# Attention and feed-forward on one core: padded 128-row scores against 64-row scores of two heads side by side

## The chip, the cores and the metric

The kernel runs on one core of a Trainium2 chip. The metric is the time of one execution on the device in microseconds (us); the median of 3 runs before the change is 449.39 us (449.11 to 452.02). Engines are named as in the profile: PE is TensorE (matmuls; PEld its weight loads), DVE is VectorE, ACT is ScalarE, POOL is GpSimd, and SP issues most transfers (DMA).

## The reference

The input is q, k, v of 8 batches, 12 heads, 448 positions, 64 columns (float32), two gains of 64, and two weights. What is computed:

```python
def rmsnorm(x, g):
    rms = np.sqrt(np.mean(x * x, axis=-1, keepdims=True) + 1e-06)
    return x / rms * g
q_n, k_n = rmsnorm(q, g_q), rmsnorm(k, g_k)
scores = (1 / 8) * q_n @ k_n.transpose(0, 1, 3, 2)
attn = softmax(scores)                      # over the keys
x = (attn @ v)  as 3584 tokens x 768        # 12 heads of 64 side by side
h = x @ w_in                                # 768 x 2048
out = (h * clip(h + 3, 0, 6) / 6) @ w_out   # 2048 x 768
```

## The kernel before

**Pairs.** Two heads, A and B, are one pair; a batch has 6, and there are 48 pairs. The 448 keys of a head are three tiles of 128 and a rest of 64. The rests of A and B share one tile, so a pair has seven key tiles: 0 to 2 of A, 3 with both rests, 4 to 6 of B.

**A pair's way.** k, q and v are loaded for two pairs at a time (`load_k`, `load_q`, `load_v`, into three rings). `square`, `stats_sum` and `stats_rstd` give the reciprocal norms on POOL or ACT, on DVE and on ACT. The first 14 pairs (`TD = 14`) are normalized on POOL or DVE (`normalize`, L333), transposed by PE (`transposes`, L349) into a PSUM tile, and copied out: `put_q` (L385, DVE or ACT) with the gains multiplied in, and `put_k` (L390) in two DVE copies of 64 rows. The later 34 pairs are normalized on POOL into a staging tile that the weights' loads have left free (`normalize_k`, L359, two operations; `normalize_q`, L367), transposed by a DMA that SP issues (`transposes_dma`, L378), and scaled by ACT (`scale_q`, L375).

**Padded k.** The transposed q of a pair holds A's 64 columns on rows 0 to 63 and B's on rows 64 to 127. The transposed k, `kpad`, has seven blocks of 128 columns. A block of A has k on rows 0 to 63 and zeros below, a block of B zeros above, the shared block both. So a score (`score`, L393) is a matmul over all 128 rows for every tile, and the zeros take the other head out. Zeros are written once (`clear_k`, `clear_kq`).

**From scores to x.** Scores go to two PSUM banks in turn; ACT makes the exponential of each (`expo`, L399) into one of 14 buffers. `weigh` (L413, L419) runs when all seven exponentials of a pair are there: in two halves, for each of four query tiles, it sums seven products with v, which has a column of ones for the denominators (the shared tile with both heads at once, 130 columns; the others 65). DVE divides (`divide`, L428, L429). The result is transposed by PE and copied by DVE (`x_out`, L446, `put_x`, L457) or, from pair 14, by DMA (L450).

**Feed-forward.** A batch whose six pairs are done gives 16 tiles of h, six matmuls of 448 columns each (`h_mm`, L461), a relu on ACT (L467) and a gate on DVE (L472), and then outputs of 16 matmuls of 384 columns (`y_mm`, L480) that ACT or DVE copies out (L280). L280 is the line of a helper, `copy`, that also casts v and the weights.

**What sets the order.** A planner in the kernel (`Plan`) plays the program through with a price for each operation on each engine that may run it, and writes out the instructions of every engine in the order that comes of it. An operation is ready a fixed time after those that it depends on; among ready ones the smallest key goes first. On PE, matmuls of attention and of the feed-forward share the time by credits; after 110 us of planned time PE's operations are put 500 ns behind what they need from other engines. Each engine then runs its own list in order, and waits on semaphores where the data asks for it.

Of the kernel before, what the change touches and what calls it, by code (L numbers as in the profile page):

```python
# [8 lines left out]
FP32 = mybir.dt.float32  # L9
BF16 = mybir.dt.bfloat16  # L10
# [35 lines left out]
class Plan:  # L46
# [52 lines left out]

    def begin(self, op, engine, ns, fn, now):  # L100
        fn()
        self.free[engine] = now + ns
        op.end = now + ns + op.lag
# [54 lines left out]
def kernel(  # L158
# [15 lines left out]
    P = 128  # L174
# [32 lines left out]
    k_st = ring(NS, [P, GP, 2, 5, D], FP32, "k_st")  # L207
    v_st = ring(NS, [P, GP, 2, 4, D], FP32, "v_st")
    vaug = ring(NV, [P, 4, 2, D + 1], BF16, "vaug")
    kq_r = ring(NK, [P, 11 * P], BF16, "kq")  # L210
    kpad = [x[:, 0:7 * P] for x in kq_r]
# [5 lines left out]
    qT_r = [x[:, 7 * P:7 * P + S] for x in kq_r]  # L217
# [7 lines left out]
    KQ = 11 * P // 2  # L225
# [37 lines left out]
    def load_k(eng, p, n):  # L263
        g, pr = part_of(p, n)
        src, st = heads(k, p, n), k_st[g][:, pr]
        eng.dma_start(
            out=st.rearrange("p r h t d -> p (r h) (t d)")[:, :, 0:NT * D], in_=blocks(src))
        for rows, x, t, rest in zip((lo, hi), (0, 0), (NT, 4), halves_of(src)):
            eng.dma_start(out=st[rows, :, x, t, :], in_=rest)
# [34 lines left out]
    def raw(a, p, n):  # L304

        g, pr = part_of(p, n)
        return (k_st, q_st)[a][g][:, pr].rearrange("p r h t d -> p r (h t) d")[:, :, 0:8, :]

    def square(eng, a, p, n, m):
        x = raw(a, p, n).rearrange("p r s d -> p r (s d)")  # L310
        sq = sq_r[m][:, 0:n].rearrange("p r s d -> p r (s d)")
# [20 lines left out]
    def normalize(eng, p, a):  # L332
        eng.tensor_tensor(  # L333
            out=qk_r[p % NQ][:, a].rearrange("p t h d -> p h t d"),
            in0=raw(a, p, 1).rearrange("p r (h t) d -> p (r h) t d", h=2),
# [19 lines left out]
    def normalize_k(eng, p):  # L355
        blocks = kq_st[p % NQ][:, 0:7 * P]
        for h in range(2):
            c0 = h * (NT * P)
            eng.tensor_tensor(  # L359
                out=blocks[:, c0:c0 + W4].rearrange("p (t c) -> p t c", t=4)[:, :, h * D:(h + 1) * D],  # L360
                in0=raw(0, p, 1)[:, 0, 4 * h:4 * h + 4, :],
                in1=rstd_r[(p // GP) % 2][:, 0, p % GP, 4 * h:4 * h + 4].unsqueeze(2)
                .to_broadcast([P, 4, D]), op=A_MULT,
            )

    def normalize_q(eng, p):
        eng.tensor_tensor(  # L367
            out=kq_st[p % NQ][:, 7 * P:11 * P].rearrange("p (t h d) -> p h t d", t=4, h=2),
            in0=raw(1, p, 1).rearrange("p r (h t) d -> p (r h) t d", h=2),
            in1=rstd_r[(p // GP) % 2][:, 1, p % GP, :].rearrange("p (h t) -> p h t", h=2)  # L370
            .unsqueeze(3).to_broadcast([P, 2, 4, D]), op=A_MULT,
        )

# [13 lines left out]
    def put_k(p, part):  # L387
        kp = kpad[p % NK]
        rows, c0 = ((lo, 0), (hi, NT * P))[part]
        nc.vector.tensor_copy(out=kp[rows, c0:c0 + 4 * P], in_=t_ps[rows, 0, :])  # L390

    def score(p, i, n):
        nc.tensor.matmul(  # L393
            out=sc_r[n % 2][:, 0:S], lhsT=kpad[p % NK][:, i * P:(i + 1) * P],
            rhs=qT_r[p % NK], start=True, stop=True,
        )
# [8 lines left out]
    def weigh(p, half):  # L405
        va = vaug[p % NV]
        e = {i: eT_r[(7 * p + n) % NE] for n, i in enumerate(ORDER)}
        for i in (2 * half, 2 * half + 1):


            c0 = i * P if (p // HP) % 2 == 0 else (i * P - P if i else S - P)
            cols = slice(c0, c0 + P)
            nc.tensor.matmul(  # L413
                out=av_ps[:, i, 0:2 * W], lhsT=e[3][:, cols], rhs=va[:, 3].rearrange("p h d -> p (h d)"),
                start=True, stop=False, skip_group_check=True,
            )
            for t in range(NT):
                for h in range(2):
                    nc.tensor.matmul(  # L419
                        out=av_ps[:, i, h * W:(h + 1) * W], lhsT=e[4 * h + t][:, cols],  # L420
                        rhs=va[:, t, h], start=False, stop=(t == NT - 1 and h == 1),
                        skip_group_check=True,
                    )
# [73 lines left out]
    def clear(eng, i):  # L497

        eng.memset(k_st[i][REST:P, :, 0, NT, :], 0.0)
        eng.memset(k_st[i][0:REST, :, 0, 4, :], 0.0)  # L500
# [5 lines left out]

    def clear_k(eng, i):
        eng.memset(kpad[i][D:P, 0:3 * P], 0.0)
        eng.memset(kpad[i][0:D, 4 * P:7 * P], 0.0)
# [15 lines left out]
    def clear_kq(eng, i):  # L525
        blocks = kq_st[i][:, 0:7 * P].rearrange("p (t c) -> p t c", c=P)
        eng.memset(blocks[:, 0:NT, D:P], 0.0)
        eng.memset(blocks[:, NT + 1:7, 0:D], 0.0)

# [6 lines left out]
    ORDER = (0, 1, 2, 3, 4, 5, 6)  # L536
# [9 lines left out]
    def x_stage(p):  # L546
        b = p // HP
        if p >= TD:
# [5 lines left out]
                      [div[p], at(px, p - 1)] + ([pq[p + 2], pk[2 * p + 4], pk[2 * p + 5]] if p >= HP else []),  # L554
                      165))
        px.append(add((p + 2, 1), [("DVE", 390, lambda: put_x(p))],
# [4 lines left out]
    def h_item(b, f):  # L561
# [7 lines left out]
        r = add((0, 0), [("ACT", 550, lambda: relu(it.bank[0], t))],  # L569
                [it.ops[-1]] + gate_ops[n - len(t_r):n - len(t_r) + 1] * (n >= len(t_r)))  # L570
        it.out = add((0, 0), [("DVE", 600, lambda: gate(b, f, it.bank[0], t))], [r])
# [217 lines left out]
```

## Time and profile before

| what | value |
|---|---|
| median of 3 runs | 449.39 us |
| profiled execution, span from the first to the last instruction | 449.5 us; the page gives no other time for it |
| first matmul begins, last one ends | 9.86 us, 445.76 us |
| scores, L393 | 336, 128 rows x 128, 448 columns, 359 ns each in the record |
| h, L461, and y, L480 | 768 and 896, 355 and 326 ns each in the record |
| values, L413 and L419 | 192 and 1152, 222 and 194 ns each in the record |
| exponentials on ACT, L399 | 336, 542 ns |
| granted PE clock, mean | 0.995 of full speed |

Matmuls are pipelined: the record of one reaches over the beginning of the next, so PE's busy time and the mean of a record say less than the distance from one beginning to the next. In the slices of the page a digit is the busy share of a fortieth of the span (11.2 us) in tenths. In the order of time a row begins with its start and its length in us; "x6" merges six equal instructions. In the table by stage the columns after the stage and its length are the busy us of PE, PEld, DVE, ACT and POOL with the number of instructions, then the granted clock, the DMA engines' share and GB/s. In the chain a row is start, length and what it was.

### The profile page before, as it was taken

How to read it: one execution, taken by the hardware profiler on the slowest of the kernel's cores; microseconds unless marked ns; L12 is line 12 of the kernel's file. 1: busy time of each engine (PE TensorE's matmuls, PEld its weight loads, DVE VectorE, ACT ScalarE, POOL GpSimd, SP SyncE). 2: the span in 40 equal slices, each digit the busy share in tenths (PEclk: the TensorE clock that was granted, in tenths of full speed). 3: DMA queues.
4: the chain of work that ended last, by engine and by line, in shares of the span. 5: the costliest groups of instructions: out<-in, count | busy, mean ns of one | idle time of the engine just before them, and what ended most of it. 6: DMA issues, size and time to landing. Idle time of an engine off the chain costs nothing.

```text
span 449.5 us, 9164 instructions
## 1 busy us (share of the span) xinstructions
PE 424.5 (94%) x3512; PEld 255.4 (57%) x3512; DVE 240.1 (53%) x428; ACT 274.8 (61%) x581; POOL 229.7 (51%) x251
## 2 busy tenths in 40 slices
PE   0888799899999989999999999999999999999996
PEld 0455366565566555666566565656565655555563
DVE  6899888845474346646444555453433253343321
ACT  2678678853487678878776777777767551132100
POOL 5899999958577766855667467552310000000000
PEclk9999899999999999999999999999999999999999
DMA  6899999981999999999899777955545210110021
GB/s 160 208 295 247 306 294 283 309 296 47 216 229 191 227 231 199 169 232 188 160 184 219 177 176 171 223 140 76 93 106 72 73 26 36 61 45 36 24 83 70
DMA packets 140908, 73.94 MB, mean 164 GB/s; under 512 B 90176, under 2 KB 137280, under 8 KB 140864
## 3 DMA queue, kind: packets, MB, share of 16 engines
q1 hardware_dynamic: 139232, 72.44, 69.3%
q10 hardware_dynamic: 1632, 0.92, 0.8%
q8 instruction: 27, 0.44, 0.4%
q14 instruction: 17, 0.14, 0.1%
HBM read 45.61 MB, written 11.01 MB: 126 GB/s over the span
## 4 chain that ended last, share of the span: by engine, by line
PE 84%; DMA 6%; POOL 2%; DVE 2%; ACT 2%; SPq 1%; issue 1%; POOLq 0%
PE m L461 29%; PE m L480 26%; PE sc L393 11%; PE av L419 7%; PE sc L480 5%; DMA k_st<-in_k_dram 4%; DMA kq<-w_st 3%; PE sc L461 3%; PE av L413 2%; ACT eT L399 2%; POOL qk L333 1%; POOL sq L315 1%; DVE vaug L280 1%; PE t_ps L349 1%; SPq L277 0%
## 5 line engine op out<-in xcount | busy, mean ns | idle before, releaser
L399 ACT ACTIVATE eT<-sc 128x448 bf16<-128x448 f32 x336 | 175.7, 542 | 48.6 <-PE sc L393 44.6
L461 PE MATMUL m<-xT,w_in_sb 128*128 128x448 bf16 x708 | 165.7, 355 | 0.2
L480 PE MATMUL m<-w_out_sb,gT 128*128 128x384 bf16 x768 | 150.0, 326 | 0.0
L393 PE MATMUL sc<-kq 128*128 128x448 bf16 x336 | 115.9, 359 | 8.2 <-ACT eT L399 6.4
L480 PEld LDWEIGHTS <-gT 128*128 128x128 bf16 x896 | 87.2, 98 | 62.3 <-issue 0.5
L461 PEld LDWEIGHTS <-w_in_sb 128*128 128x128 bf16 x768 | 74.1, 98 | 68.8 <-issue 6.0
L472 DVE SCALAR_TENSOR_TENSOR gT<-t_sb,m 128x448 bf16<-128x448 f32 x118 | 73.0, 620 | 72.9 <-ACT t_sb L467 72.4
L467 ACT ACTIVATE t_sb<-m 128x448 f32<-128x448 f32 x118 | 63.7, 541 | 47.3 <-PE m L461 44.3
L318 DVE TENSOR_REDUCE ssq<-sq 128x16 f32<-128x1024 f32 (+1 forms) x56 | 58.3, 1058 | 8.4 <-POOL sq L315 7.1
L359 POOL TENSOR_TENSOR w_st<-k_st,rstd 128x256 bf16<-128x256 f32 x68 | 40.2, 612 | 41.3 <-DMA kq<-w_st 40.6
L280 DVE COPY y_sb<-m 128x384 f32<-128x384 f32 x39 | 21.7, 557 | 61.4 <-PE m L480 61.2
L419 PE MATMUL av<-vaug,eT 128*128 128x65 bf16 x1152 | 54.5, 194 | 0.0
L419 PEld LDWEIGHTS <-eT 128*128 128x128 bf16 x1152 | 50.8, 99 | 4.4 <-issue 0.4
L315 POOL TENSOR_TENSOR sq<-k_st 128x1024 f32<-128x1024 f32 (+1 forms) x24 | 42.4, 1765 | 12.7 <-DMA k_st<-in_k_dram 5.9
L315 POOL TENSOR_TENSOR sq<-q_st 128x1024 f32<-128x1024 f32 (+1 forms) x26 | 44.5, 1710 | 7.1 <-DMA q_st<-in_q_dram 3.5
L393 PEld LDWEIGHTS <-kq 128*128 128x128 bf16 x336 | 31.3, 99 | 27.0 <-issue 4.9
L413 PE MATMUL av<-vaug,eT 128*128 128x130 bf16 x192 | 42.7, 222 | 0.0
L280 POOL CAST vaug<-v_st 128x512 bf16<-128x512 f32 x29 | 17.9, 618 | 45.2 <-PE av L419 44.6
L367 POOL TENSOR_TENSOR w_st<-q_st,rstd 128x512 bf16<-128x512 f32 x34 | 35.4, 1042 | 0.0
L429 DVE TENSOR_TENSOR xn<-av,rden 128x512 bf16<-128x512 f32 x48 | 33.2, 691 | 1.7
L428 DVE RECIPROCAL rden<-av 128x8 f32<-128x8 f32 x48 | 9.8, 205 | 34.1 <-PE av L419 33.7
L375 ACT ACTIVATE kq<-kq,gprime 128x448 bf16<-128x448 bf16 x34 | 22.6, 663 | 5.1 <-DMA kq<-w_st 5.1
(55 smaller groups left out, 222.5 us busy)
## 6 DMA issues: line engine op xcount, KB each, us to landing
out_dram<-y_sb SPq DMA_DIRECT2D x24, 384.0 KB, 2.9
k_st<-in_k_dram SPq DMA_DIRECT2D x23, 384.0 KB, 4.6
v_st<-in_v_dram SPq DMA_DIRECT2D x23, 384.0 KB, 4.6
q_st<-in_q_dram SPq DMA_DIRECT2D x22, 384.0 KB, 4.7
w_st<-in_moe_w_in_dram SPq DMA_DIRECT2D x8, 768.0 KB, 7.6
w_st<-in_moe_w_out_dram SPq DMA_DIRECT2D x8, 768.0 KB, 7.1
out_dram<-y_sb SPq DMA_DIRECT2D x8, 192.0 KB, 2.7
k_st<-in_k_dram SPq DMA_DIRECT2D x46, 32.0 KB, 3.9
```

Source lines behind the costliest of these rows:

```text
L280: (eng.copy if eng is nc.scalar else eng.tensor_copy)(out=out, in_=in_)
L315: eng.tensor_tensor(out=sq, in0=x, in1=x, op=A_MULT)
L318: nc.vector.tensor_reduce(out=ssq_r[(p // GP) % 2][:, a, p % GP:p % GP + n, :].rearrange("p r s -> p (r s)"), in_=sq_r[m][:, 0:n].rearrang ...
L359: eng.tensor_tensor(out=blocks[:, c0:c0 + W4].rearrange("p (t c) -> p t c", t=4)[:, :, h * D:(h + 1) * D], in0=raw(0, p, 1)[:, 0, 4 * h:4 ...
L393: nc.tensor.matmul(out=sc_r[n % 2][:, 0:S], lhsT=kpad[p % NK][:, i * P:(i + 1) * P], rhs=qT_r[p % NK], start=True, stop=True,)
L399: nc.scalar.activation(out=eT_r[n % NE][:, 0:S], in_=sc_r[n % 2][:, 0:S], func=EXP, bias=0.0, scale=1.0,)
L413: nc.tensor.matmul(out=av_ps[:, i, 0:2 * W], lhsT=e[3][:, cols], rhs=va[:, 3].rearrange("p h d -> p (h d)"), start=True, stop=False, skip_ ...
L419: nc.tensor.matmul(out=av_ps[:, i, h * W:(h + 1) * W], lhsT=e[4 * h + t][:, cols], rhs=va[:, t, h], start=False, stop=(t == NT - 1 and h = ...
L461: nc.tensor.matmul(out=m[:, 0:S], lhsT=w_in_sb[:, kt, f * P:(f + 1) * P], rhs=xT[:, kt, b % NX, x_slot(b)], start=(kt == 0), stop=(kt == N ...
L467: nc.scalar.activation(out=t[:], in_=m[:, 0:S], func=RELU, bias=0.5, scale=1.0 / 6.0,)
L472: nc.vector.scalar_tensor_tensor(out=gT[:, f, (b % 2) * S:(b % 2 + 1) * S], in0=t[:], scalar=1.0, in1=m[:, 0:S], op0=A_MIN, op1=A_MULT,)
L480: nc.tensor.matmul(out=m[:, 0:n], lhsT=gT[:, f, c0:c0 + P], rhs=w_out_sb[:, f, c:c + n], start=(f == 0), stop=(f == NFT - 1),)
```

## The change

k is no longer padded. Its transpose is four blocks of 128 columns, with A on rows 0 to 63 and B on rows 64 to 127, and the rests of both in the fourth. A score of A is a matmul over rows 0 to 63 alone, one of B over rows 64 to 127, and the shared tile over all. The order of the key tiles becomes shared, A0, B0, A1, B1, A2, B2. For pairs 14 to 47 the planner issues A's and B's score of one tile as one step into the two banks; for the first 14 pairs each score stays a step of its own. `weigh` handles one key tile for all four query tiles, so a pair's values are seven steps, each after its own exponential, in place of two after all seven. Scores have the first key on PE. `put_k` is one copy of 128 rows, on DVE or ACT; the late k is normalized in one operation; the clears of padding are gone; the transposing DMA moves 8 blocks in place of 11. The planner's prices are changed too, and a fixed delay per engine (`LAG`) is added to the end of an operation.

```diff
+    LAG = {"POOL": 45, "ACT": 105, "DVE": 85}
-        op.end = now + ns + op.lag
+        op.end = now + ns + (op.lag or self.LAG.get(engine, 0))
...
-    kq_r = ring(NK, [P, 11 * P], BF16, "kq")
-    kpad = [x[:, 0:7 * P] for x in kq_r]
+    kq_r = ring(NK, [P, 8 * P], BF16, "kq")
...
-    def put_k(p, part):
-        kp = kpad[p % NK]
-        rows, c0 = ((lo, 0), (hi, NT * P))[part]
-        nc.vector.tensor_copy(out=kp[rows, c0:c0 + 4 * P], in_=t_ps[rows, 0, :])
+    def put_k(eng, p):
+        copy(eng, out=kq_r[p % NK][:, 0:W4], in_=t_ps[:, 0, :])
 
     def score(p, i, n):
+        if i == NT:
+            rows, c0 = slice(0, P), i * P
+        else:
+            rows, c0 = ((lo, i * P), (hi, (i - 4) * P))[i > NT]
         nc.tensor.matmul(
-            out=sc_r[n % 2][:, 0:S], lhsT=kpad[p % NK][:, i * P:(i + 1) * P],
-            rhs=qT_r[p % NK], start=True, stop=True,
+            out=sc_r[n % 2][:, 0:S], lhsT=kq_r[p % NK][rows, c0:c0 + P],
+            rhs=qT_r[p % NK][rows, :], start=True, stop=True,
         )
...
-    def weigh(p, half):
+    def weigh(p, n):
+        va, i = vaug[p % NV], ORDER[n]
+        e = eT_r[(7 * p + n) % NE]
+        first, last = n == 0, n == len(ORDER) - 1
+        for j in range(4):
...
+            if i == NT:
+                out, rhs = av_ps[:, j, 0:2 * W], va[:, NT].rearrange("p h d -> p (h d)")
+            else:
+                h, t = divmod(i, 4)
+                out, rhs = av_ps[:, j, h * W:(h + 1) * W], va[:, t, h]
             nc.tensor.matmul(
+                out=out, lhsT=e[:, c0:c0 + P], rhs=rhs,
+                start=first and j % 2 == 0, stop=last, skip_group_check=True,
             )
...
-    ORDER = (0, 1, 2, 3, 4, 5, 6)
+    ORDER = (3, 0, 4, 1, 5, 2, 6)
...
-        vc.append(add((p, 5), [("DVE", 700, lambda p=p: cast_v(V, p)),
-                               ("POOL", 640, lambda p=p: cast_v(G, p)),
-                               ("ACT", 640, lambda p=p: cast_v(A_, p))],
+        vc.append(add((p, 5), [("DVE", 1350, lambda p=p: cast_v(V, p)),
+                               ("POOL", 575, lambda p=p: cast_v(G, p)),
+                               ("ACT", 530, lambda p=p: cast_v(A_, p))],
...
-            scs.append(add((p, 2), [("PE", 189, lambda p=p, i=i, m=m: score(p, i, m))],
-                           [pq[p], pk[2 * p], pk[2 * p + 1] if i >= 3 else None, at(exs, m - 2)], 165))
+            if p < TD or n == 0:
+                scs.append(add((-1, p), [("PE", 189, lambda p=p, i=i, m=m: score(p, i, m))],
+                               [pq[p], pk[p], at(exs, m - 2)], 165))
+            elif n % 2:
+                both = [(i, m), (ORDER[n + 1], m + 1)]
+                scs += 2 * [add((-1, p), [("PE", 300, lambda p=p, both=both: [score(p, *x) for x in both])],
+                                [pq[p], pk[p], exs[m - 2], exs[m - 1]], 165)]
...
-        for half in range(2):
-            wgh.append(add((p + 1, 1), [("PE", 510, lambda p=p, half=half: weigh(p, half))],
-                           exs[7 * p:7 * p + 7] + [vc[p], at(div, p - 1), pad], 165))
+        for n in range(7):
+            wgh.append(add((p + 1, 1), [("PE", 240 if ORDER[n] == NT else 132, lambda p=p, n=n: weigh(p, n))],
+                           [exs[7 * p + n], vc[p], at(div, p - 1), pad, wgh[-1] if n else None], 165))
```

137 lines of the change are left out of this document (48 added, 89 removed).

## The prediction

> **What bounds the kernel now.** I read the page's shares and its 40 slices first, then the busy time by stage, then PE in order of time, then the costliest groups, then the chain that ended last.
>
> The page, shares of the span and the slices:
>
> ```profile
> PE 424.5 (94%) x3512; PEld 255.4 (57%) x3512; DVE 240.1 (53%) x428; ACT 274.8 (61%) x581; POOL 229.7 (51%) x251
> ...
> PE   0888799899999989999999999999999999999996
> ...
> PEclk9999899999999999999999999999999999999999
> ```
>
> No other engine is above 61%, and PE falls below 9 tenths only in the first slices. The same by stage (busy us of PE, PEld, DVE, ACT, POOL; clock; DMA share):
>
> ```profile
> 0.00:56.00 56.00, 37.62 (x364) 22.06 (x365) 47.69 (x103) 36.28 (x86) 48.19 (x68) 0.97 0.89 243
> 56.00:146.00 90.00, 88.64 (x791) 54.92 (x790) 58.51 (x104) 60.26 (x130) 71.05 (x63) 1.00 0.94 234
> 146.00:366.00 220.00, 218.48 (x1882) 132.72 (x1880) 105.42 (x174) 163.67 (x340) 110.48 (x121) 1.00 0.78 160
> 366.00:450.00 84.00, 79.76 (x488) 45.69 (x485) 28.46 (x49) 14.55 (x27) 0.00 (x0) 0.99 0.14 49
> ```
>
> From 56 us on PE has no room; before that DVE and POOL are busy 48 of 56 us. What PE's time consists of is seen in the order of time:
>
> ```profile
> 38.42 0.61 PE L349 MATMUL t_ps<-identity,qk 128*128 128x128 bf16 x8
> 38.86 0.35 PE L393 MATMUL sc<-kq 128*128 128x448 bf16 x1
> ...
> 202.09 0.35 PE L419 MATMUL av<-vaug,eT 128*128 128x65 bf16 x6
> 202.29 0.22 PE L413 MATMUL av<-vaug,eT 128*128 128x130 bf16 x1
> ...
> 207.20 0.35 PE L393 MATMUL sc<-kq 128*128 128x448 bf16 x1
> 207.39 1.11 PE L461 MATMUL m<-xT,w_in_sb 128*128 128x448 bf16 x5
> 208.34 0.35 PE L393 MATMUL sc<-kq 128*128 128x448 bf16 x1
> ```
>
> A record of 448 columns lasts 0.35 us, but the next begins 0.19 us later (207.20 to 207.39; five in 0.95 us): pipelined, one costs 189 ns and its tail of 166 ns lies under its successor. In the same way a 384-column matmul costs 162.5 ns (the chain has 16 in 2.60 us), six 65-column ones 0.20 us (33 ns each), a 130-column one 52 ns, a 128-column transpose 55 ns (eight in 0.44). The sum: 768 x 0.189 + 896 x 0.1625 + 336 scores x 0.189 + 192 x 0.25 for the values + 9.6 for transposes = 412 us. The span is 449.5; of the other 37.5, 9.9 lie ahead of the first matmul, 3.7 behind the last (the last copy and store), and 24 are gaps and slow clock before 56 us. The span is 0.1 above the 449.39 of the runs, so I add nothing.
>
> **The change part by part.**
>
> *Scores, 34 late pairs (14 to 47).* Seven scores of 0.189 a pair become one full one and three groups of two on 64 rows each. In the order of the changed kernel's PE instructions all 102 groups stand back to back, between full-height matmuls, so each is one entry into half-height tiles and one exit. Now two scores cost 0.378. Together they cost 0.189 plus the offset of the second, plus the toll of entry and exit. No row shows a half-height tile, so both are bounded. The offset lies between 0 and 0.189 (no overlap); I take 33 ns, the closest spacing of two separately loaded matmuls (L419). The toll lies between 0 (from transposes to scores, 38.42 to 38.86, eight take 0.44 and nothing is added) and 2 x (166 ns tail + 98 ns weight load) = 0.53 us. I take the time the array needs to run empty: at 189/448 = 0.42 ns a column, and assuming a row takes as long, 128 rows on entry are 54 ns (L349's 55 ns for 128 columns) and 64 rows on exit 27 ns: 81 ns. A group is then 0.189 + 0.033 + 0.081 = 0.303, 75 ns less than now: 102 x 0.075 = **-7.6 us**.
>
> For two matmuls on different row groups the Trainium skill ("TensorE: Matmul & The Clock Gate", Part 3, The mechanism) gives starts about 4 ns apart. No run here shows it yet; by it the sum would be 3.0 us lower, 439.7.
>
> *Scores, 14 early pairs.* They are ordered singly as the exponentials free the banks. Pairs 7 to 13 have 40 runs of half-height scores, hence 40 tolls, and only two adjacent couples: 40 x 0.081 - 2 x 0.156 = **+2.9**, in a stage where PE has no room. Pairs 0 to 6 have 33 tolls, 2.7 us; scores there wait for ACT anyway, so I count a third, **+0.9** (2.7 if that cover is gone).
>
> *Start.* Who holds up the feed-forward there is read in the chain:
>
> ```profile
> 32.45 5.26 DMA k_st<-in_k_dram
> 37.71 1.40 DVE vaug L280
> ...
> 42.73 0.68 DVE vaug L280
> 43.45 2.05 DVE vaug L280
> ...
> 46.33 0.70 DVE xn L429
> ...
> 48.76 0.40 DVE xT L457
> 49.21 3.15 PE m L461 x8
> ```
>
> From 37.7 to 47 us the chain is on DVE, and 4.1 us of it are casts of v; the first long run of feed-forward starts when the sixth xT is done. In the changed order DVE casts no v at all (its 10 casts and three of ACT's 9 go to POOL, whose 29 become 42), put_k is one copy instead of two of 417 ns, four put_q and one put_k go to ACT. DVE's chain loses up to 4.1 + 0.4. But POOL takes more (0.62 us a cast) and is itself full from 22 to 34 us, and DMA is busy at a share of 0.9 in this stage. Bounds: -4.5 (all of it) and +3.7 (six more casts in POOL's way before 56 us). I take **-3.0**; what is late next is POOL's normalizing and the k load at 32.45.
>
> *Values.* The same 192 + 1152 matmuls in seven steps of four instead of two blocks of 14; four of one key tile cost 4 x 33 or 4 x 52 ns as before: **0**. Each step adds a wait for its own exponential, and PE executes in order, so everything behind it would wait; the steps stand one to seven feed-forward matmuls (0.2 to 1.3 us) behind the scores, which covers an exponential of 0.54. Without that cover see the fourth rival.
>
> *Off the path.* The late k is one POOL operation instead of two of 612 ns; the transposing DMA moves 8 blocks instead of 11; the clears of padding go. POOL is busy half of 146 to 366 us, and its longest wait is for that DMA (40.6 us in all): **0**, hidden behind PE. Behind the last values stand 33 feed-forward matmuls (5.4 us) before the last batch is needed; division (0.2 + 0.69) and transposing DMA (1.2 + 2.8) take 4.9: **0**, up to +1 if that DMA is slow. Changed planner prices move work, not amounts.
>
> Sum: -7.6 + 2.9 + 0.9 - 3.0 = -6.8; 449.5 - 6.8 = **442.7**.
>
> **The rivals.**
>
> *Free switch.* Nothing is lost at entry or exit. For it: transposes follow scores without a gap. Against: they use the whole array. -102 x 0.156 - 0.3 - 3.0 = -19.2: 430.
>
> *Weights can't be loaded across a switch (slower).* Now every weight load is hidden under the matmul ahead (PEld overlaps PE). If the array must be empty before the new height's weights go in, each of 350 switches exposes a load of 98 ns; a toll is 0.196. A group is 0.418: 102 x 0.040 = +4.1; early pairs 40 x 0.196 - 0.3 = +7.5; first pairs +2.2; start -3.0: +10.8, 460. If the 166 ns tail is exposed at each switch instead, the toll is 0.332 and the sum +18.0 + 13.0 + 3.7 - 3.0 = +31.7, 481. It decides from where 153 tolls (102 + 40 + a third of 33) eat the 19.2 us: a toll of 126 ns. Against it: that the trace never shows a weight load uncovered by form; for it: no record has a change of height.
>
> The Trainium skill ("TensorEngine Tiling (Array Packing)", Key Properties) says that a change of tiling mode drains the engine, without a duration. By a drain to the end of the record the time would be this rival's 481; no row here shows such a switch.
>
> *The two halves don't run together.* The second score streams behind the first: a group is 0.378 + 0.081, +8.3; early +3.2; +0.9; -3.0: +9.4, 459. For it: all matmuls in the trace start in sequence; against: none is on half the rows.
>
> *A new wait for both banks.* A group needs both score banks, so both exponentials of the group before. Between groups stand typically 4 + 4 value and 9 feed-forward matmuls, 1.7 us; the tail 0.17, two exponentials 0.98 and a relu between 0.44 need 1.6. If 0.1 is missing at each of 102, +10.2 - 6.8: 453. Against: after 56 us PE waited for exponentials only 2.6 us in all.
>
> **How the numbers follow.** Forecast 0.38 (its own range 437 to 448); free switch 0.13; exposed weight load 0.28, exposed tail 0.08; no overlap 0.07; bank wait 0.06. Predicted 442.7. One per cent is 4.5 us, about what a measurement here tells from no change. Faster by more: 0.13 + 0.27 of the forecast = 0.40. Within: 0.11 of the forecast + 0.04 from low tolls of the second rival = 0.15. Slower: 0.45. The cases of both signs weigh alike, so the range goes from the free switch to beyond the exposed load, 429 to 465; outside lie the exposed tail and the rims, some 0.17.
>
> **What would show it.** In PE's order of time: the second score of a group starting about 33 ns after the first (0.19 if they don't run together); the next full matmul 0.22 to 0.25 us after the group's first; the matmul ahead of a group 0.05 longer than its 0.16 or 0.19 (0.1 or more by the second rival). In the stages: the sixth xT near 46 us; waits of scores for exponentials still under 5 us after 56 us. A toll above 126 ns, or PE waiting at the groups, would make the forecast wrong.

## The result, and the profile after

The changed kernel takes **465.7 us** (median of 4 runs, 465.22 to 465.94) against 449.52 us (449.11 to 452.02) beside it: a ratio of 1.033, interval 1.0294 to 1.0366. It is 16.2 us slower. Its profiled execution took 465.22 us with a span of 463.4, so 1.8 us lie around the span. The kernel before has 1.7 to 1.9 us around its span in every later run that lists both. Its traced execution, with a span of 449.5, therefore took about 451.3 us (an estimate) and was one of its longer ones. The prediction took this span for a time and added nothing. That it came out at the median all the same is luck: two differences of nearly 2 us cancel. The sums below are made from medians.

The page of the changed kernel, shares and slices:

```profile
PE 443.8 (96%) x3512; PEld 237.9 (51%) x3512; DVE 219.5 (47%) x390; ACT 276.1 (60%) x587; POOL 224.1 (48%) x223
...
PE   0899989999999999999999999999999999999996
...
PEclk9999999999999999999999999999999999999999
```

PE has the same 3512 matmuls and is busy 19.3 us longer, while DVE and POOL got lighter as the change meant. From the third slice to the fifth PE is now at 9 tenths, where before it was at 8, 8 and 7. The table by stage (busy us and number of instructions of PE, PEld, DVE, ACT, POOL; granted clock; DMA share; GB/s):

```profile
0.00:56.00 56.00, 42.48 (x295) 20.76 (x296) 28.02 (x72) 35.54 (x80) 37.00 (x61) 1.00 0.81 226
56.00:146.00 90.00, 88.75 (x722) 48.00 (x721) 52.59 (x91) 54.89 (x117) 66.61 (x54) 1.00 0.76 208
146.00:366.00 220.00, 218.92 (x1854) 117.00 (x1851) 105.46 (x172) 152.92 (x327) 119.86 (x108) 1.00 0.68 155
366.00:464.00 98.00, 93.67 (x646) 52.15 (x644) 33.47 (x59) 32.74 (x65) 0.62 (x1) 1.00 0.18 53
```

The counts in the second column tell where the time went. Up to 56 us PE began 295 matmuls instead of 364, although it was busy 42.48 us instead of 37.62. From 56 to 146 us it began 722 instead of 791, equally busy; from 146 to 366, 1854 instead of 1882. So two losses of 69 matmuls each lie in the first 146 us, and one of 28 in the 220 us of the late pairs, for which the change was meant. At the mean cost of a matmul in the prediction's sum, 412 us / 3512 = 0.117 us, that is roughly 8, 8 and 3 us.

What a group costs is seen where one stands between full-height matmuls. PE in order of time, then its weight loads at the same place:

```profile
181.35 1.11 PE L447 MATMUL m<-xT,w_in_sb 128*128 128x448 bf16 x5
182.39 0.36 PE L381 MATMUL sc<-kq 64*128 64x448 bf16 x2
182.68 0.93 PE L447 MATMUL m<-xT,w_in_sb 128*128 128x448 bf16 x4
```

```profile
181.32 0.69 PEld L447 LDWEIGHTS <-w_in_sb 128*128 128x128 bf16 x5
182.38 0.10 PEld L381 LDWEIGHTS <-kq 64*128 64x128 bf16 x2 [0.37 <-issue]
182.68 0.49 PEld L447 LDWEIGHTS <-w_in_sb 128*128 128x128 bf16 x4 [0.20 <-issue]
```

The two scores really run together: both lie in one record length of 0.36 us, and their starts in the trace, 182.387 and 182.390, are 3 ns apart. But five h matmuls ahead of them take 1.04 us instead of 5 x 0.189 = 0.945, and the next h begins 0.29 us after the couple instead of 0.19. In ns: 96 on entry, 103 on exit, a **toll of 199 ns**. A group costs 0.391 us, where two full-height scores cost 0.378. The weight loads show where this time lies. Elsewhere the loads run ahead of the matmuls: five in a row are done after 0.69 us, under matmuls that take 1.04. At both switches the load waits (0.37 and 0.20 us, put down to "issue") and begins 4 ns ahead of its own matmul.

The second finding is in the start, PE in order of time:

```profile
29.99 0.55 PE L381 MATMUL sc<-kq 64*128 64x448 bf16 x1
30.48 0.40 PE L406 MATMUL av<-vaug,eT 128*128 128x65 bf16 x4
30.81 0.55 PE L381 MATMUL sc<-kq 64*128 64x448 bf16 x1
...
46.70 0.58 PE L381 MATMUL sc<-kq 128*128 128x448 bf16 x1
...
47.46 0.36 PE L381 MATMUL sc<-kq 64*128 64x448 bf16 x1
```

A record of a score lasts 0.55 to 0.58 us up to 47 us and 0.36 from there on. Half-speed records are also what before shows at its beginning, but there they end at 21.5 us (and come back from 49.2 to 52.2, the eight h in 3.15 us that the prediction quoted). The clock row of the page does not show this: it stands at 9 throughout, and the table by stage has 1.00 before 56 us. The chain that ended last, which before 47 us ran over DVE's casts of v, now runs over PE there:

```profile
42.89 0.48 PE sc L381
43.37 0.34 PE av L406 x4
43.71 0.48 PE sc L381
44.19 0.78 PE av L406 x12
44.97 0.48 PE sc L381
45.45 0.86 PE m L447 x2
```

### The profile page after: what moved, and what is told of

It is laid out like the page before. It is cut to its first block, busy times and chain, and to the rows that moved or that the text cites. A ratio compares the mean times of both kernels' runs of the same rounds, so it can differ in the third digit from the quotient of the medians.

```text
span 463.4 us, 9088 instructions
## 1 busy us (share of the span) xinstructions
PE 443.8 (96%) x3512; PEld 237.9 (51%) x3512; DVE 219.5 (47%) x390; ACT 276.1 (60%) x587; POOL 224.1 (48%) x223
## 4 chain that ended last, share of the span: by engine, by line
PE 91%; DMA 3%; ACT 2%; DVE 1%; SPq 1%; issue 0%; POOL 0%; DVEq 0%; ACTq 0%; POOLq 0%
PE m L447 30%; PE m L466 28%; PE sc L381 13%; PE av L406 12%; PE sc L466 3%; DMA k_st<-in_k_dram 2%; PE t_ps L354 2%; PE sc L447 1%; ACT eT L387 1%; DMA gk_t<-in_g_k_dram 1%; PE m L432 0%; PE t_ps L432 0%; SPq L270 0%; SPq L267 0%; ACT t_sb L453 0%
## 5 line engine op out<-in xcount | busy, mean ns | idle before, releaser
L387 ACT ACTIVATE eT<-sc 128x448 bf16<-128x448 f32 x336 | 171.1, 542 | 88.6 <-PE sc L381 86.0
L406 PEld LDWEIGHTS <-eT 128*128 128x128 bf16 x1344 | 79.7, 100 | 56.9 <-issue 25.2
L406 PE MATMUL av<-vaug,eT 128*128 128x65 bf16 (+1 forms) x1344 | 102.6, 202 | 0.5 <-ACT eT L387 0.4
L466 PEld LDWEIGHTS <-gT 128*128 128x128 bf16 x896 | 78.8, 98 | 44.3 <-issue 3.6
L381 PE MATMUL sc<-kq 64*128 64x448 bf16 (+1 forms) x336 | 89.9, 379 | 4.1 <-DVE kq L281 2.6
L447 PEld LDWEIGHTS <-w_in_sb 128*128 128x128 bf16 x768 | 65.4, 98 | 48.2 <-issue 9.1
L281 POOL CAST vaug<-v_st 128x512 bf16<-128x512 f32 x42 | 25.9, 618 | 93.7 <-PE av L406 93.4
L381 PEld LDWEIGHTS <-kq 64*128 64x128 bf16 (+1 forms) x336 | 21.8, 94 | 53.7 <-issue 44.1
L338 POOL TENSOR_TENSOR w_st<-k_st,rstd 128x512 bf16<-128x512 f32 x34 | 35.4, 1042 | 15.4 <-DMA kq<-w_st 15.1
L354 PE MATMUL t_ps<-identity,qk 128*128 128x128 bf16 x112 | 11.2, 258 | 9.7 <-POOL qk L338 9.7
```

Of the source, the lines that this page charges most:

```text
L281: (eng.copy if eng is nc.scalar else eng.tensor_copy)(out=out, in_=in_)
L338: eng.tensor_tensor(out=out, in0=raw(a, p, 1)[:, 0], in1=rstd_r[(p // GP) % 2][:, a, p % GP, :].rearrange("p (h t) -> p h t", h=2) .unsque ...
L381: nc.tensor.matmul(out=sc_r[n % 2][:, 0:S], lhsT=kq_r[p % NK][rows, c0:c0 + P], rhs=qT_r[p % NK][rows, :], start=True, stop=True,)
L387: nc.scalar.activation(out=eT_r[n % NE][:, 0:S], in_=sc_r[n % 2][:, 0:S], func=EXP, bias=0.0, scale=1.0,)
L406: nc.tensor.matmul(out=out, lhsT=e[:, c0:c0 + P], rhs=rhs, start=first and j % 2 == 0, stop=last, skip_group_check=True,)
L447: nc.tensor.matmul(out=m[:, 0:S], lhsT=w_in_sb[:, kt, f * P:(f + 1) * P], rhs=xT[:, kt, b % NX, x_slot(b)], start=(kt == 0), stop=(kt == N ...
```

## The experiments

In seven of the kernels scores read all 128 rows of unpadded k and q in some pairs, so the products of A and B are added up there; each expectation says in which. Each ratio is against the kernel before, run beside it on the same chip.

| kernel | median us | ratio to before | interval |
|---|---|---|---|
| full_all: full-height scores in all pairs | 446.28 | 0.9905 | 0.9874 to 0.9935 |
| full_early: full-height in pairs 0 to 13 | 448.88 | 0.9967 | 0.9943 to 0.9991 |
| full_late: full-height in pairs 14 to 47 | 462.61 | 1.0248 | 1.0191 to 1.0305 |
| full_but_7to13: half-height in pairs 7 to 13 alone | 452.64 | 1.0053 | 1.0031 to 1.0076 |
| full_first2: full-height in pairs 0 and 1 alone | 455.47 | 1.0112 | 1.0089 to 1.0134 |
| padded_new_order | 450.88 | 1.0019 | 0.9996 to 1.0042 |
| before_half | 499.79 | 1.1087 | 1.1005 to 1.1168 |
| late_twice | 467.32 | 1.0375 | 1.0345 to 1.0405 |
| tolls_alone | 461.72 | 1.0260 | 1.0146 to 1.0374 |
| early_twice | 484.34 | 1.0763 | 1.0707 to 1.0818 |
| after_warm | 467.45 | 1.0370 | 1.0332 to 1.0407 |
| before_warm | 453.59 | 1.0070 | 1.0038 to 1.0102 |
| grouped_warm | 455.22 | 1.0104 | 1.0073 to 1.0135 |
| runs_of_four | 447.79 | 0.9932 | 0.9908 to 0.9956 |

### Which pairs lose the time

All pairs at full height, with the order, the copies and the transfers of the changed kernel:

```diff
     def score(p, i, n):
...
             rows, c0 = ((lo, i * P), (hi, (i - 4) * P))[i > NT]
+            if True:
+                rows = slice(0, P)
```

> The changed kernel with its order, prices, copies and transfers untouched; every score alone reads all 128 rows of the unpadded k and q, so that A's and B's products are added up in it (this part of the computation is changed; the time of everything else is as before). Toll theory (entry into and exit from half-height tiles cost PE 0.199 us, read from the changed kernel's trace): no tolls at all. The 102 late groups go from 0.391 to 0.378 (-1.3), the 40 early runs lose 0.199 each (-8.0), and the first pairs lose theirs (up to -6): 450 to 456, against 465.7. Order theory (seven value steps, new prices and waits cost the time): stays above 462. Slow-clock theory (half-height scores keep PE at half speed until 47 us): full speed from some 21 us on, as in the kernel before.

It gave 446.28, below the lower end of what was expected: with half height taken away, everything else in the change is worth 4.1 us (446.28 against 450.4). The first stages of this kernel:

```profile
0.00:56.00 56.00, 37.66 (x388) 22.70 (x389) 35.90 (x84) 43.57 (x102) 46.72 (x69) 1.00 0.87 240
56.00:146.00 90.00, 88.57 (x777) 54.62 (x775) 52.81 (x89) 54.80 (x120) 68.78 (x56) 1.00 0.91 239
```

At 56 us it is 24 matmuls ahead of before (388 against 364), about 24 x 0.117 = 2.8 us. So the start did get shorter. Lighter DVE work (35.90 us up to 56 us, before 47.69) is one cause at hand. The clock is another: here records are at full speed from 16.5 us, before from 21.5, and the second slow stretch that before shows from 49.2 us does not come. No run separates the two.

The same edit with `if p < TD:`, full height in the early pairs only:

> The changed kernel, full 128-row scores (heads added up, so this part of the computation is changed) in the first 14 pairs alone; the late 34 pairs keep their half-height groups. Toll theory: 8.0 us from pairs 7 to 13 and up to 6 from pairs 0 to 6 go away, the 102 late groups stay at 0.391: 451 to 458, about 1.3 above the kernel with full scores everywhere. Order theory: above 462. Slow-clock theory: full speed from about 21 us on, so most of the gain lies before 56 us.

448.88: the 102 late groups cost 448.88 - 446.28 = 2.6 us. Their measured tolls explain 102 x (0.391 - 0.378) = 1.3; the other 1.3 is within what the two medians leave uncertain, and the trace shows where it may lie. In four of the 102 groups the second score starts late, by 0.07 to 0.64 us and by 1.5 us in all, because the exponential that frees its bank is not done. PE in order of time at one of the longest two:

```profile
181.57 0.36 PE L383 MATMUL sc<-kq 64*128 64x448 bf16 x1
182.22 0.35 PE L383 MATMUL sc<-kq 64*128 64x448 bf16 x1 [0.28 <-ACT eT L389]
```

The idle time of 0.28 us is less than the delay of 0.64, because the record of the first score covers the rest.

The opposite, `if p >= TD:`:

> The changed kernel, full 128-row scores (heads added up, so this part of the computation is changed) in the late 34 pairs alone; the first 14 pairs keep their single half-height scores. Toll theory: only 102 x (0.391 - 0.378) = 1.3 us go away, 463 to 465, and the records of the first 60 us look as in the changed kernel, half speed until 47 us. If instead the late groups are what costs: 452 to 456.

462.61: half height in the 14 early pairs alone costs 462.61 - 446.28 = 16.3 us. The loss is here, not in the late pairs.

Within the early pairs, `if p < 7 or p >= TD:`, half height in pairs 7 to 13 alone:

> The changed kernel with half-height scores in pairs 7 to 13 alone, full ones (heads added up, so this part of the computation is changed) elsewhere. The start and the late pairs are those of the kernel with full scores everywhere (446.3), so the difference is the price of 40 single runs in a stage without room on PE. Toll theory: +7.6, 453.9 (452.5 to 455.5). If the tolls there are hidden beside other waits: 446 to 449.

452.64, 6.4 above full_all. With 40 runs of half-height scores that is 0.16 us each; 40 tolls of 199 ns are 8.0, less 2 x 0.19 for the two couples that overlap, 7.6. The two medians leave about 1 us uncertain, so the tolls are enough to explain it.

And `if p < 2:`, only the first two pairs at full height:

> The changed kernel with full 128-row scores (heads added up, so this part of the computation is changed) in pairs 0 and 1 alone. It separates PE's slow clock at the start from the tolls. Slow-clock theory: with the first 14 scores at full height PE reaches full speed near 16 us, as with all early scores full, and keeps it; what stays against the kernel with all early scores full (448.9) are the tolls of pairs 7 to 13 (40 x 0.199 - 2 x 0.186 = 7.6) and those of pairs 2 to 6 (25 x 0.199 = 5.0, part of it beside waits for ACT): 456 to 461.5. If half-height scores themselves hold the clock down, half speed returns or stays until about 47 us: 463 to 465.5.

455.47: the first two pairs alone are worth 465.70 - 455.47 = **10.2 us**. PE in order of time in this kernel:

```profile
29.06 0.36 PE L383 MATMUL sc<-kq 64*128 64x448 bf16 x1
29.36 0.30 PE L408 MATMUL av<-vaug,eT 128*128 128x65 bf16 x4
29.58 0.36 PE L383 MATMUL sc<-kq 64*128 64x448 bf16 x1
29.88 0.30 PE L408 MATMUL av<-vaug,eT 128*128 128x65 bf16 x4
```

The same half-height scores of pairs 2 to 6 now last 0.36 us, and a score with its four values takes 0.52 us instead of 0.82. Full-speed records begin at 21.1 us instead of 47.3. Pairs 2 to 6 then cost next to nothing: 455.47 - 448.88 - 6.4 = 0.2 us, give or take 1. Yet 25 tolls stand in them, 25 x 0.199 = 5.0 us. Before 56 us PE is idle 15.0 us here and 18.0 in full_early, so most of these tolls seem to fill time in which PE would have waited anyway.

### What the order and the lighter copies are worth without half height

k padded again as before, with the new key order, the values tile by tile and the changed prices:

```diff
-    kq_r = ring(NK, [P, 8 * P], BF16, "kq")
+    kq_r = ring(NK, [P, 11 * P], BF16, "kq")
+    kpad = [x[:, 0:7 * P] for x in kq_r]
...
-    def put_k(eng, p):
-        copy(eng, out=kq_r[p % NK][:, 0:W4], in_=t_ps[:, 0, :])
+    def put_k(eng, p):
+        for rows, c0 in ((lo, 0), (hi, NT * P)):
+            copy(eng, out=kpad[p % NK][rows, c0:c0 + 4 * P], in_=t_ps[rows, 0, :])
```

> The same result as the reference: padded k as in the kernel before (two copies of 64 rows on DVE, two POOL operations for the late k, 11 blocks by the transposing DMA), with the changed kernel's key order, values key tile by key tile, score pairs as one step, and prices. Order theory turned round (the new order is a gain of its own, which the half-height scores ate): 446 to 449, since the second put_k copy costs DVE 14 x 0.417 = 5.8 us in a stage where DVE is half idle in the changed kernel. If the cheap copies of the unpadded k made the gain of the kernel with full scores everywhere: 450 to 453.

450.88 against 450.66, no difference. The stages say that the start gained even more than in full_all, and where that went:

```profile
0.00:56.00 56.00, 37.62 (x405) 23.79 (x406) 40.53 (x98) 43.03 (x98) 46.68 (x71) 1.00 0.87 239
...
146.00:366.00 220.00, 214.62 (x1826) 128.25 (x1825) 102.96 (x169) 154.73 (x330) 113.22 (x126) 1.00 0.74 157
```

It is 41 matmuls ahead of before at 56 us, but from 146 to 366 us PE is idle 5.4 of 220 us, where before it is idle 1.5. The largest of these waits is for a transposing DMA:

```profile
159.89 0.35 PE L460 MATMUL m<-xT,w_in_sb 128*128 128x448 bf16 x1 [2.07 <-DMA xT<-xn]
```

So the gain at the start was given back later. In full_all, with 8 blocks a pair to transpose in place of 11, PE is idle 1.2 us in that stage. Smaller transfers may be the reason, but no run changed them alone, and the kernel before, which also moves 11 blocks, is idle no more than 1.5 us there. So the new order and the 11 blocks together are a possible reading, not a shown one.

### Is the price one of the switch, and per run?

The kernel before with one edit: its score reads the 64 rows that hold k, from the same padded buffer, in the same order, so no score has a partner on the other half.

```diff
     def score(p, i, n):
+        rows = slice(0, P) if i == NT else (lo, hi)[i > NT]
         nc.tensor.matmul(
-            out=sc_r[n % 2][:, 0:S], lhsT=kpad[p % NK][:, i * P:(i + 1) * P],
-            rhs=qT_r[p % NK], start=True, stop=True,
+            out=sc_r[n % 2][:, 0:S], lhsT=kpad[p % NK][rows, i * P:(i + 1) * P],
+            rhs=qT_r[p % NK][rows, :], start=True, stop=True,
```

> The kernel before, order and padding untouched; only its scores of A read rows 0 to 63 and those of B rows 64 to 127 (the same result, the zeros are not read). In its order almost every half-height score stands alone: 224 runs after pair 6, 18 before. Toll theory: 224 x 0.199 = 44.6 us more, and up to 4 from the first pairs: 494 to 500; with a slow clock at the start up to 505. Free switch with another cause of the loss: 449 to 455.

499.79, as expected of tolls of 0.2 us: its 224 runs of half-height scores make 224 x 0.199 = 44.6 of the 49.4 us; slow records until 34.5 us are there too.

Next, full_early with each late group issued twice, as A, B, A, B:

```diff
-                scs += 2 * [add((-1, p), [("PE", 300, lambda p=p, both=both: [score(p, *x) for x in both])],
+                scs += 2 * [add((-1, p), [("PE", 300, lambda p=p, both=both: [score(p, *x) for x in both + both])],
```

> Full early scores as in the earlier run (heads added up in the first 14 pairs), and each late group of two issued twice in a row (A, B, A, B; the second writing the same values again), so that a run has four half-height scores in place of two. Toll theory, toll per run: 448.9 + 102 x 0.189 = 468.2 (467 to 471). If every change between the halves also pays, or the two halves of the second couple do not overlap: 478 to 490.

467.32, 18.4 above full_early, which is 18.4 / 102 = 0.181 us for a second couple: the price of one score, without another toll. The same place as above, PE in order of time:

```profile
181.71 0.73 PE L449 MATMUL m<-xT,w_in_sb 128*128 128x448 bf16 x3
182.38 0.55 PE L383 MATMUL sc<-kq 64*128 64x448 bf16 x4
182.86 0.30 PE L408 MATMUL av<-vaug,eT 128*128 128x65 bf16 x4
```

Four half-height matmuls stand 0.48 us ahead of the next full one, 0.19 more than two. Going from rows 0 to 63 to rows 64 to 127 and back is free; only a change of height is paid for.

### What keeps PE at half speed

Three accounts were open: half-height work does not raise the clock; the tolls, empty PE time, do not; or the clock only lacks a first push. First the push, 90 matmuls of 128 columns ahead of everything in the changed kernel:

```diff
+        for _ in range(90):
+            nc.tensor.matmul(out=m_r[0][:, 0:P], lhsT=identity[:], rhs=identity[:], start=True, stop=True)
         plan.run()
```

> The changed kernel, with 90 matmuls of the identity by itself put ahead of all others on PE (into a bank that nothing uses yet), so that PE has work from about 2 us, while it waits for the first loads; the result is the same. Slow-clock theory: the price of half speed until 47 us is the difference of the changed kernel and the one with full scores in pairs 0 and 1, 465.7 - 455.5 = 10.2; if the early work brings PE to full speed and the half-height scores then hold it: 453 to 457. If half-height scores let it fall back to half speed: 463 to 466.

467.45, no gain. In the table by stage of this kernel the granted clock of the start can be read, since the early push left clock records:

```profile
0.00:12.00 12.00, 7.98 (x98) 7.46 (x98) 5.79 (x26) 3.68 (x8) 4.58 (x27) 1.00 0.58 154
12.00:49.00 37.00, 33.79 (x201) 15.71 (x201) 16.27 (x33) 23.92 (x54) 26.93 (x28) 0.51 0.88 250
49.00:60.00 11.00, 10.23 (x109) 5.43 (x109) 7.90 (x16) 10.38 (x24) 7.91 (x9) 0.96 0.77 226
```

Records were at full speed from 5.6 us to the last transposes at 10.4. Then PE waited 3.3 us for the first transposed k, and with the scores behind it the clock was at 0.51 for 37 us, in which PE was busy 91% by its records. This also confirms that records of 0.55 us mean half the clock. The Trainium skill ("TensorE: Matmul & The Clock Gate", Part 1) lets the clock come up after about 3.4 us of sustained work. The kernel before fits that loosely, with full speed from 21.5 us; these 37 us do not, so here "sustained work" cannot mean only that a matmul is in progress.

The same 90 matmuls ahead of the kernel before:

> The kernel before with the same 90 matmuls ahead (same result). Its PE runs at half speed until 21 us and once more from 49 to 52 us. If only the first stretch goes: work of 21 - 10 us at half speed, of which much lies beside waits for loads: 0 to 3 us less than before, 447.5 to 450.5. If PE's speed there is hidden behind DVE and POOL: no change.

453.59 against 450.75, slower instead of faster: full speed came at 20.5 us, one microsecond earlier than without them, and the third score began at 15.04 instead of 13.77 us behind a wait of 1.95 for an exponential instead of 0.45. ACT runs its list in order, and ahead of that exponential it has a square of k, which began at 13.92 us instead of 12.65. Its wait of 1.64 us is put down to POOL's normalizing there, and in the kernel before to a load of k (0.51 us). Why POOL comes into it is open.

And with the early pairs grouped like the late ones as well, so that they have fewer switches:

```diff
-            if p < TD or n == 0:
+            if n == 0:
...
-            if n == 0 or p < TD or n % 2 == 0:
-                for x in range(m if n == 0 or p < TD else m - 1, m + 1):
+            if n == 0 or n % 2 == 0:
+                for x in range(m if n == 0 else m - 1, m + 1):
```

> As the run before it, and A's and B's score of one tile issued as one step in the first 14 pairs too (same result). Toll theory: 40 runs between pairs 7 and 13 become 21 groups at 0.391 against 0.378, so of the 6.4 us that the single runs cost there (452.6 against 446.3) 6.1 go away: 447 to 451. If pairing holds up the exponentials there, since a group waits for both banks: 453 or more.

455.22: 10.5 us better than the changed kernel and 12.2 better than the push alone. Full speed comes back at 27.2 us, with the early half-height scores still there but in couples that use both row halves at once; fewer switches is the other difference. It misses the expected time of 447 to 451. Two things seen in the trace go with that: PE waits 2.3 us for exponentials before 60 us instead of 0.2, since a couple needs two of them, and the slow clock comes back from 47.7 to 51.1 us.

Last, the two causes apart. Full-height scores in the early pairs, and ahead of each of the 84 a half-height matmul of only 64 columns into the unused rest of the bank, so that the switches stay and the half-height work goes:

```diff
+            if p < TD:
+                rows = slice(0, P)
+        if p < TD and i != NT:
+            half = (lo, hi)[i > NT]
+            nc.tensor.matmul(
+                out=sc_r[n % 2][:, S:S + REST], lhsT=kq_r[p % NK][half, c0:c0 + P],
+                rhs=qT_r[p % NK][half, 0:REST], start=True, stop=True,
+            )
```

> Full 128-row early scores as in the earlier run (heads added up in the first 14 pairs, so this part of the computation is changed), and ahead of each of the 84 that were half-height a half-height matmul of 64 columns into a part of the bank that is not read: the tolls of the changed kernel without its half-height work. If it is the half-height work that keeps PE slow at the start: full speed near 16 to 20 us, and 40 to 42 tolls with 27 ns of streaming between pairs 7 and 13, 448.9 + 42 x 0.226 = 458.4 (456 to 461). If the tolls, in which PE stands empty, keep it slow: half speed until 40 us or later, 464 to 470.

It took 461.72 us (two runs, 459.70 and 463.73), just above the first range. PE in order of time:

```profile
22.08 0.56 PE L389 MATMUL sc<-kq 128*128 128x448 bf16 x1
...
23.14 0.20 PE L385 MATMUL sc<-kq 64*128 64x64 bf16 x1
23.27 0.36 PE L389 MATMUL sc<-kq 128*128 128x448 bf16 x1
```

Full speed from 22.5 us, with all the switches in place. The tolls do not hold the clock down; they cost their time (12.8 us above full_early, give or take 2, for 84 switches into and out of half height and 84 small matmuls).

The opposite: the changed kernel with each early half-height score issued twice, more half-height work for each switch.

```diff
-        nc.tensor.matmul(
+        for _ in range(2 if p < TD and i != NT else 1):
+            nc.tensor.matmul(
```

> The changed kernel with each half-height score of the first 14 pairs issued twice in a row on the same rows (the second writing the same values): more half-height work, no more tolls. If PE's speed follows the time in which it has any work: full speed well ahead of 47 us. If half-height work is what keeps it slow: 47 us or later, since there is more of it. The time says little (40 x 0.189 = 7.6 more between pairs 7 and 13, and 33 x 0.37 at half speed before): 470 to 485 with the slow start, 466 to 472 without.

It took 484.34 us. PE in order of time:

```profile
54.21 0.93 PE L382 MATMUL sc<-kq 64*128 64x448 bf16 x2
55.07 0.93 PE L448 MATMUL m<-xT,w_in_sb 128*128 128x448 bf16 x2
```

At 54 us the records still show half speed (two matmuls of 448 columns in 0.93 us, 0.38 from start to start), up to 58 us. Denser half-height work does not bring the clock up. That it came up 11 us later than in the changed kernel is less telling, since the doubled scores delay everything behind them. In the four kernels that order their early half-height scores like the changed one, full speed came 1.9 to 3.7 us after the first h matmul, which is full-height work: at 47.3 us after 45.4 in the changed kernel, 48.9 after 45.4 in full_late, 58.7 after 55.1 here, 49.9 after 46.4 in after_warm. The h matmuls are not the only work that can bring it up, since in before_half and grouped_warm full speed came ahead of them (34.7 and 27.2 us). That is what the runs show. How the chip weighs the rows of a matmul when it grants the clock, none of them shows.

### A version that wins

Since the toll is per run, longer runs pay. This kernel keeps the early pairs padded and at full height, and from pair 16 on gives the scores four banks (the third bank of the feed-forward and the PSUM tile of the early transposes join the two). A late pair then has two runs in place of three: A0, B0, A1, B1 together, and A2, B2.

```diff
+    TL = TD + 2
+    four = [sc_r[0], sc_r[1], m_r[2], t_bank]
+    def bank(n):
+        return four[(n - 7 * TL) % 4] if n >= 7 * TL else sc_r[n % 2]
...
+        if p < TD:
+            runs = [(n,) for n in range(7)]
+        elif p < TL:
+            runs = [(0,), (1, 2), (3, 4), (5, 6)]
+        else:
+            runs = [(0, 1, 2, 3), (4, 5, 6)]
```

> The same result as the reference, built from what the earlier runs gave: padded full-height scores in the first 14 pairs (three copies of 64 rows on DVE for put_k in place of one), unpadded half-height scores later, and from pair 16 on four score banks (one of the feed-forward's and the idle transpose bank join), so that a pair has one run of four half-height scores (A0 B0 A1 B1) and one of two with the shared tile behind it. Toll theory, prices from the earlier runs: a run of four 0.391 + 0.181 = 0.572 against 0.756 at full height, so a pair 1.152 in place of 1.362: 32 x 0.21 = 6.7 less than the kernel with full early scores and groups of two (448.9), plus 0 to 2 for the copies: 442 to 444.5, below both kernels. If two banks are too few for the feed-forward, or a run waits for four exponentials: 449 or more.

**447.79 us, ratio 0.9932** (0.9908 to 0.9956): 3.6 us below the kernel before that ran beside it, 17.9 below the changed one. This is a small gain, but clear of the noise. It falls short of the 442 to 444.5 that were expected. A part of that lies in the feed-forward, which has two banks left and now waits for its own evacuation:

```profile
167.79 0.54 PE L458 MATMUL m<-xT,w_in_sb 128*128 128x448 bf16 x2 [0.82 <-DVE gT L469]
...
177.06 0.54 PE L458 MATMUL m<-xT,w_in_sb 128*128 128x448 bf16 x2 [0.79 <-DVE gT L469]
```

From 146 to 366 us PE is idle 5.4 us here, against 1.7 in full_early; the trace puts 3.1 us behind seven such waits for the gate, and 1.4 us behind one exponential.

## Why the prediction was wrong

The forecast was 442.7 us and a gain of 6.8; the time was 465.7, a loss of 16.2 and just above the range's 465. Term by term, from the runs:

| term | predicted us | measured us | from |
|---|---|---|---|
| 102 late groups | -7.6 | +2.6 | full_early less full_all |
| pairs 7 to 13 | +2.9 | +6.4 | full_but_7to13 less full_all |
| pairs 0 to 6 | +0.9 | +10.2 (the first two), +0.2 (the rest) | changed kernel less full_first2, and the remainder |
| start and all off PE | -3.0 | -4.1 | full_all less before |
| sum | -6.8 | +15.3 | direct: +16.2 |

The direct difference and the sum are 0.9 us apart. The kernels were timed in several sessions, and the median of the kernel before moved between 449.5 and 451.4 from one to the next, so each line is uncertain by about 1 us and nothing is to be read from the 0.9.

**Step that failed first: the toll of 81 ns.** That each change of height costs PE time was right. The reason given for the size was not: the time that the array needs to run empty, 54 ns on entry for 128 rows and 27 on exit for 64. Measured are 96 and 103 ns. That is the second rival, the weights that can't be loaded across a switch, whose toll was to be 196 ns. Three things speak for it. The size fits: the exposed loads last 93 ns on entry and 96 on exit. They begin only 4 ns ahead of their own matmul at each switch. And at half clock, where a matmul takes twice as long from start to start, they last 102 and 105 ns, and the toll grows about as little (below). Why the load has to wait, no run shows. The prediction's argument against this rival, that the trace never shows an uncovered load, could not bear on it, since the trace of before had no switch; the prediction said so and still gave the rival less weight than the forecast. The toll of 126 ns from which it was to decide is well below the measured 199, and without the slow start the change would still have lost 16.2 - 10.2 = 6.0 us.

Its record of signs in the trace: the next full matmul was to come 0.22 to 0.25 us after the group's first, and came after 0.295; the matmul ahead was to be 0.05 longer, and 0.1 by the rival, and was 0.096 longer.

**The offset of 33 ns** was too large: 3 ns. The Trainium skill's 4 ns ("TensorE: Matmul & The Clock Gate", Part 3, The mechanism) agrees with the trace, and the third rival, two halves that run one behind the other, is refuted. This error made the late groups 102 x 30 ns = 3 us dearer in the sum than they are; the toll made them 102 x 118 ns = 12 us cheaper.

**Step that failed second: "scores there wait for ACT anyway, so I count a third".** This was the cover for pairs 0 to 6, and its stated price if gone was 2.7 us. In the changed kernel it was gone: PE waits 0.2 us for exponentials before 60 us, where before it waited 3.8, because PE itself became the bound. But the price was neither 0.9 nor 2.7: the whole stage ran at half clock for 26 us longer, 10.2 us by full_first2. At full clock the cover held, since in full_first2 the 25 tolls of pairs 2 to 6 cost 0.2 us, give or take 1. So what the term lacked is the clock, which it put at nothing. This error of 9.5 us is nearly as large as that of the late groups (10.2), and no rival had it. The second rival's 460 had the toll right, and its 2.2 us for the first pairs is the term by which it came out too low. The prediction knew of slow clock, it put "gaps and slow clock" into one remainder of 24 us, but never asked what ends the slow clock, and whether the change would touch that.

**The start of -3.0** came out near by luck: with scores at full height PE is 24 matmuls ahead at 56 us, and 4.1 us are gained with all that goes along. The way named for it is not what is seen, and the clock has an unmeasured part in it. The sixth xT, predicted near 46 us, came at 59.33 in the changed kernel, and at 49.22 in full_all against 48.76 before. In the changed kernel the gain is buried: the chain there no longer runs over DVE.

**Values, 0, and the bank wait.** The steps of four at their exponentials cost next to nothing: in the changed kernel PE was idle from 56 us on for 0.4 us ahead of values and 0.6 us ahead of scores:

```profile
PE sc L381 <- ACT eT L387: 0.6, 2, 0.3
```

Second scores that start late add 1.5 us in full_early, where the fourth rival had 10.2. This refutes that rival at its price, though such waits exist, and confirms the prediction's sign of less than 5 us.

**The drain.** The Trainium skill ("TensorEngine Tiling (Array Packing)", Key Properties) says that a change of tiling mode drains the engine. The trace agrees in that a change costs time, and gives the duration: 199 ns for a change there and back. It does not go to the end of the 166 ns tail of a record, by which the prediction had 481.

## What to carry to other kernels

Half-height matmuls on two row halves do run at the same time, but each change of height between them and full ones cost 0.1 us here, where weights weren't loaded ahead across it. With 448 columns a couple is worth less than nothing (0.391 us against 0.378), a run of four pays (0.572 against 0.756), and a single one is a plain loss. Count runs in the order that PE really executes, not pairs in the source. And where a start is at half clock, ask what brings the clock up; here it was enough to keep the scores of the first two pairs at full height.

## What the runs showed of the hardware that was not expected

- PE stayed at half speed while its stream consisted of half-height scores, transposes and values: until 47.3 us in the changed kernel, 58.7 us with the scores doubled, and 37 us at a granted clock of 0.51 after an early push. With full-height scores in the first two pairs it was at full speed from 21.1 us, and the half-height scores that followed did not lose it.
- The page's clock row is filled with full speed ahead of the first clock record. In the changed kernel it reads 9 where matmuls of 448 columns last 0.55 us instead of 0.36. The length of a known record is the better clock.
- The toll depends little on the clock: in the changed kernel 0.12 to 0.14 us on entry and 0.11 on exit at half speed, 0.096 and 0.103 at full speed, while a score at half speed takes 0.373 us from start to start instead of 0.189. The weight loads at the switches change as little, from 93 and 96 ns to 102 and 105.
- Changing between rows 0 to 63 and 64 to 127 added nothing to the 0.181 us of a second couple in late_twice, and the toll is the same beside h, y and value matmuls.
